# Longer GpSimd pieces in a fused recurrence and highway layer: up to 2,048 columns instead of 512, with a new list of operations

## The chip, the cores and the metric

The kernel runs on one core of a Trainium2 chip. The metric is the device time of one execution in microseconds. TensorE, VectorE, ScalarE, GpSimd and SyncE are the engines; the profile calls them PE (PEld for its weight loads), DVE, ACT, POOL and SP.

## What is computed

The input is 4 sequences of 6,336 tokens with 256 channels. A gated recurrence runs along each sequence, and a highway layer follows on all 25,344 tokens:

```python
sig = 1.0 / (1.0 + np.exp(-f_logit))
f = lower_bound + (1.0 - lower_bound) * sig
i = 1.0 - f
for t in range(S):
    h = f[:, t] * h + i[:, t] * x[:, t]
    y[:, t] = h
# on all tokens, with x = y
H = np.maximum(x @ w_h, 0.0)
T = 1.0 / (1.0 + np.exp(-(x @ w_t + b_t)))
out = T * H + (1.0 - T) * x
```

All inputs and the output are fp32 in DRAM.

## The kernel before

**Units.** The tokens are cut into 28 units in order (`units`, L42): two of 256 tokens, one of 512, twenty-three of 1,024, then 512 and 256. A unit has up to 8 blocks of 128 tokens. A tile first has tokens on the 128 partitions; for the recurrence it is turned, so that channels lie on the partitions (two halves of 128 channels, h = 0 and 1) and tokens along the columns.

**Operations.** Each has a letter, and a token of the list such as `b5.2:1` names the operation, the unit, a part of it and the buffer slot.

- `l`, `x` (L266, L269): loads of f_logit and x, issued by SyncE; six slots each.
- `u` (L272): ScalarE, sigmoid(-f_logit), fp16.
- `b` (L278, product at L283): u times x, into bv (bf16, two blocks interleaved). In pieces of 512 columns, four to a full unit; on GpSimd, or on VectorE where the token ends in v.
- `i` (L286): TensorE transposes u into PSUM (uT). `f` (L292): ScalarE makes f from it (L300), or VectorE with v (L298).
- `p` (L303, L309): TensorE transposes bv into PSUM (bT).
- `s` (L322, L326): VectorE's scan, y = f times the last y + bT, for 128 channels and a whole unit; it starts from the last column of the unit before. Where a sequence begins inside a unit there are two scans.
- `z`, `g` (L348, L351): TensorE's products of y with the two weight matrices (L343, L141). `t` (L354, L356): ScalarE, sigmoid of z. `d` (L358, L360): VectorE, one pass that reads y and g. In `y` the recurrence stands divided by a factor per channel, which diag and the scaled weights put back.
- `E`, `e` (L367, L370, product at L365): e = d times t over the 2 × tokens columns of the unit (both halves one behind the other). Columns below the last number of the unit's row in `units` are GpSimd's (`E`, pieces of 512), the rest VectorE's (`e`, one instruction).
- `o` (L376): TensorE turns four blocks back to tokens on partitions, summing y times diag (L384) and e times the identity (L385) in PSUM. `c` (L388): copy to SBUF, ScalarE (L394) or VectorE with v (L392). `w` (L398): store, issued by SyncE.

**Order.** The string `order` (L72 to L125) is the program: its tokens are emitted one after another, and each engine, SyncE's queue included, executes its own in that order. Semaphores make a token wait for its inputs and for its slot.

**GpSimd and VectorE.** `shared` (L204) adds one more wait. It is called with every VectorE product that has two SBUF inputs (`e`, `b` with v, the weight scaling at the start), and with every GpSimd product; the first GpSimd product listed behind such a VectorE instruction waits until that one is done.

```python
    def shared(ins, gpsimd):

        if not gpsimd:
            held[:] = [ins]
        elif held:
            tc.add_manual_dep(ins.ins, held.pop().ins.name, mybir.DependencyInfo(
                mybir.DependencyClass.Sync, mybir.DependencyReason.DATA), reason="shared port")
```

Of the kernel before, what the change touches and what calls it, by code (L numbers as in the profile page):

```python
# [19 lines left out]
def kernel(  # L20
# [70 lines left out]
g10.1:0 w7.1 i13.1:1 d10.1:2 b12.1 p11.1:0 s11.1 u15:2 g10.0:2 E9.2 o9.1:1 o9.0:0 f13.1:2 x15:2 E8.0 l14:3 b13.0:1
i12.0:1 b13.2 c9.1:1 w7.0 b13.3 i15.1:0 z11.0:1 b15.1:2 f12.0:0 p12.0:1 d10.0 z10.0:2 c9.0:2 x14:3 t11.0:0 o8.0:0
f15.1v:1 t10.0 w9.0 p12.1:0 b13.1 o8.1:2 s12.0:2 g11.1:1 c8.0:3 s12.1 i13.0:1 u14:0 E10.0:2 z12.1:0 b15.0 w9.1 d11.1:0
p13.1:0 z11.1:1 f13.0:0 i14.1:1 c8.1:0 e10 b14.1:0 w8.0 s13.1:0 g11.0:2 b14.2 t12.1:2 t11.1 l16:4 z12.0:0 b14.3
f14.1:3 w8.1 b14.0 x16:4 g12.0:1 t12.0 i14.0:0 p13.0:1 f14.0:2 d11.0 o10.0:2 d12.0:1 o10.1:1 c10.0:2 s13.0 l17:5
g12.1:0 E11.2:0 E11.0 E11.1 i15.0:1 p14.1:0 d12.1 c10.1:1 u16:1 z13.0:2 g13.0:0 e12:1 t13.0:1 f15.0:0 s14.1:1 o11.0:1
c11.0:3 E11.3 z13.1:2 p14.0:1 b16.3:1 b15.2 t13.1 b15.3 i16.0:0 f16.0:3 o11.1:1 d13.0:2 b16.0 g13.1:2 i16.1:0 w10.1
s14.0 c11.1:0 w10.0 p15.1:1 l20:0 d13.1 u17:0 w11.0 x17:5 b16.1 E12.0 s15.1:3 f16.1:2 z14.1:1 z14.0:0 b16.2 g14.1:2
d14.1:0 p15.0:1 l19:1 w11.1 i17.1:0 t14.1:0 E13.2:2 E13.3 s15.0 o12.1:2 E13.1 t14.0 g14.0:0 l18:2 x19:0 x18:1 u20:2
o12.0:1 c12.1:1 w12.1 d14.0 E13.0 p16.0:1 z15.0:2 b17.1:0 l21:3 f17.1:1 b17.0 b17.3 c12.0:2 E14.2:0 p16.1:0 t15.0:2  # L100
b17.2 s16.0:2 o13.1:1 g15.0:0 E14.1 i17.0:1 u19:1 o13.0:2 s16.1 f17.0:0 d15.0:1 p17.0:0 s17.0:0 g16.0:0 c13.0:3
c13.1:0 p17.1:1 u18:0 z15.1:1 E14.0 z16.1:2 E14.3 d16.0:2 i19.1:0 s17.1 g16.1:0 t15.1 w12.0 w13.0 x21:3 g15.1:1 d15.1
f19.1:3 w13.1 i18.0:0 i20.0:1 b19.1:2 b19.3 t16.1:1 g17.0:2 x20:2 b18.2:1 f18.0:2 i18.1:0 o14.0:1 b18.0 d16.1 d17.0:0
b18.3 b18.1 e15:1 E15.1 g17.1:0 o14.1:2 d17.1 b19.2 E15.0 f20.0:0 f18.1:1 c14.0:1 p18.1:1 u21:0 z16.0:1 z17.0:0
s18.1:1 t16.0 p18.0:0 o15.1:1 t17.0:0 b19.0 s18.0 b21.2:0 o15.0:0 c14.1:2 p19.1:1 z17.1:2 c15.1:3 e16:2 E17.1:0
b20.1:1 c15.0:0 i19.0:0 z18.1:1 b20.0 b20.3 l22:4 t17.1 b20.2 w14.0 g18.0:0 f19.0:1 z18.0:2 w14.1 p19.0:0 s19.1:3
E17.3 i20.1:1 d18.0:1 w15.1 t18.1:2 t18.0 o16.1:1 E17.0 g18.1:2 o16.0:0 b21.1 s19.0 d18.1 f20.1:2 w15.0 p20.0:1
i21.1:0 c16.1:1 z19.0:1 c16.0:2 E17.2 f21.1:3 x22:4 g19.1:0 b21.0 u22:1 b21.3 s20.0:2 z19.1:2 p20.1:0 i22.0:1 d19.1:2
s20.1 l23:5 t19.0:1 g19.0:0 o17.0:1 i21.0:0 f22.0:1 w16.1 t19.1 e18:1 g20.1:2 c17.0:3 f21.0:0 w16.0 d19.0 p21.0:1
o17.1:1 b22.1:2 b22.3 E19.1:2 d20.1:0 u23:2 p21.1:0 E19.2 z20.0:0 s21.0:0 o18.0:2 c17.1:0 t20.0:0 b22.0 z20.1:1  # L110
i23.1:1 x23:5 s21.1 b22.2 g20.0:0 c18.0:1 t20.1 o18.1:2 f23.1:2 d20.0 l24:0 p22.0:0 c18.1:2 w17.0 s22.0:1 i22.1:1
g21.0:1 z21.1:0 f22.1:0 i23.0:1 u24:0 b23.2:1 b23.1 p22.1:0 z21.0:2 d21.0:1 t21.1:2 E19.3 s22.1 g21.1:1 b23.0 E19.0
# [3 lines left out]
g23.1:1 c20.0:2 s24.1:2 i25.0:0 b25.3 z23.0:0 f25.0:3 z23.1:2 E21.1 i25.1:0 w20.1 b25.2 p24.0:1 t23.0:0 g23.0:0 t23.1
d23.1:0 o21.0:2 E22.0:2 w20.0 o21.1:1 E22.2 f25.1:2 c21.0:3 s24.0 E22.1 p25.0:0 x27:2 d23.0 c21.1:0 z24.0:2 x26:3
E22.3 z24.1:1 u26:2 s25.0:0 g24.1:0 p25.1:1 t24.0:2 d24.1:1 s25.1 t24.1 i26.0:0 f26.0:0 o22.0:2 o22.1:1 E23.0:0
g24.0:0 i26.1:0 b26.1:1 c22.0:1 b26.0 c22.1:2 d24.0 u27:0 z25.0:2 i27.0:1 e23 e24:1 g25.0:1 f26.1:1 z25.1:0 d25.0:2
w21.0 t25.0:1 E24.0 p26.1:0 o23.0:2 f27.0:3 E24.1 p26.0:1 o24.0:1 t25.1 w22.0 g25.1:0 c23.0:3 w21.1 b27.0:0 s26.1:1  # L120
# [71 lines left out]
    def tokens(n):  # L192
        return units[n][1] * units[n][2]

    def pieces(n):

        at, N = units[n][3], tokens(n)
        cuts = [0] + [c - at for c in firsts if at < c < at + N] + [N]
        return [(at + c in firsts, c, e) for c, e in zip(cuts, cuts[1:])]
# [240 lines left out]
```

## Time and profile before

The time before is 210.31 us (median of 3 runs, 210.30 to 210.35). The profile is of one execution whose span, from the first to the last instruction, is 208.8 us; 1.5 us lie around it.

| group | engine | count | mean ns of one |
|---|---|---|---|
| bv of 512 columns, L283 | GpSimd | 96 | 1,179 |
| e of 512 columns, L365 | GpSimd | 54 | 1,168 |
| scan of 1,024 tokens, L326 | VectorE | 40 | 2,336 |
| d of 1,024 tokens, L360 | VectorE | 46 | 1,263 |
| e of 2,048 / 1,536 / 1,024 / 512 columns, L365 | VectorE | 4 / 4 / 5 / 3 | 1,208 / 984 / 758 / 459 |
| bv of 512 columns, L283 | VectorE | 3 | 731 |
| copy o of 512 columns, L392 | VectorE | 1 | 665 |
| copy o of 1,024 columns, L394 | ScalarE | 48 | 1,057 |
| f of 1,024 tokens, L300 | ScalarE | 45 | 1,164 |
| u of 2,048 columns, L275 | ScalarE | 23 | 1,954 |

A mean is the length of one record. Records of one engine overlap a little, so the distance from one start to the next is shorter (a scan of 2,336 ns is followed 2.26 us after its start). The busy time counts overlapping time once. Lines of the profile's groups read: line, engine, operation, output <- inputs, shape, count | busy us, mean ns | idle time of the engine just before them, with what ended it. Lines of a timeline read: start, length, engine, line, operation, count, and in brackets the idle time before it. A digit in the slices is the busy share of a fortieth of the span, in tenths.

### The profile page before, as it was taken

The page shows a single profiled execution, that of the slowest core. Times are in us where ns is not written, and L with a number is a line of the kernel's source. Part 1 is how long each engine was busy: PE and PEld are TensorE (multiplying, and loading weights), DVE is VectorE, ACT ScalarE, POOL GpSimd, SP SyncE. Part 2 cuts the span into 40 slices and gives each one's busy share as a digit, 9 for nine tenths or more (in the row PEclk, how much of TensorE's full clock was granted, in tenths as well). Part 3 has the DMA queues.
Part 4 walks back from the last instruction along what each step waited for, and adds up shares of the span by engine and source line. Part 5 has one row for each costly group of instructions (what it writes and reads, how often), then busy time and mean ns, then how long its engine had stood idle before and what let it go on. Part 6 is the DMA issues. An engine that isn't in the chain of part 4 may idle for free.

```text
span 208.8 us, 4668 instructions
## 1 busy us (share of the span) xinstructions
PE 192.3 (92%) x1827; PEld 132.6 (64%) x1827; DVE 194.4 (93%) x154; ACT 195.0 (93%) x191; POOL 171.7 (82%) x162
## 2 busy tenths in 40 slices
PE   7888787989999999999999989999999999999991
PEld 2355455577675765776675766777677577776870
DVE  0799998999999999999999999999999999999970
ACT  4769979999999999999999999999999999999882
POOL 3076989789999399998799999879979988997920
PEclk9999999999999999999999999999999999999997
DMA  5999999999999999999999999999998999926676
GB/s 230 391 427 414 416 422 424 414 410 425 415 426 409 419 399 336 392 417 317 425 413 403 417 416 421 432 408 421 421 428 350 342 372 400 333 110 257 248 296 258
DMA packets 15982, 78.69 MB, mean 377 GB/s; under 512 B 1748, under 2 KB 2264, under 8 KB 10072
## 3 DMA queue, kind: packets, MB, share of 16 engines
q1 hardware_dynamic: 15952, 78.39, 93.6%
q8 instruction: 14, 0.23, 0.4%
q14 instruction: 8, 0.07, 0.1%
q10 hardware_dynamic: 8, 0.00, 0.0%
HBM read 52.43 MB, written 25.95 MB: 375 GB/s over the span
## 4 chain that ended last, share of the span: by engine, by line
PE 44%; DMA 17%; DVE 15%; ACT 12%; issue 5%; POOL 3%; SPq 2%; ACTq 0%; DVEq 0%; POOLq 0%
DMA l<-in_f_logit_dram 13%; DVE y L326 9%; PE op L385 6%; PE z L343 6%; PE op L384 6%; PE g L343 6%; PE z L141 5%; PE bT L309 5%; PE uT L289 5%; PE g L141 5%; DVE d L360 4%; ACT f L300 4%; DMA x<-in_x_dram 4%; ACT o L394 3%; ACT u L275 2%
## 5 line engine op out<-in xcount | busy, mean ns | idle before, releaser
L283 POOL TENSOR_TENSOR bv<-u,x 128x512 bf16<-128x512 f16 x96 | 110.3, 1179 | 21.7 <-DMA x<-in_x_dram 9.6
L326 DVE TENSOR_TENSOR_SCAN y<-f,y,bT 128x1024 bf16<-128x1024 f16 (+5 forms) x54 | 106.7, 1991 | 1.1 <-ACT f L300 0.5
L365 POOL TENSOR_TENSOR e<-d,t 128x512 bf16<-128x512 bf16 (+1 forms) x55 | 62.5, 1159 | 7.6 <-DVE e L365 4.5
L360 DVE SCALAR_TENSOR_TENSOR d<-y,ncc,g 128x1024 bf16<-128x1024 bf16 (+2 forms) x56 | 63.0, 1140 | 1.1 <-PE g L343 0.9
L300 ACT ACTIVATE f<-uT,ncc 128x1024 f16<-128x1024 f16 (+2 forms) x53 | 56.4, 1073 | 3.0 <-PE uT L289 2.9
L356 ACT ACTIVATE t<-z,bt 128x1024 bf16<-128x1024 f32 (+2 forms) x56 | 57.2, 1060 | 0.6 <-PE z L141 0.2
L394 ACT COPY o<-op 128x1024 f32<-128x1024 f32 (+1 forms) x50 | 50.7, 1038 | 2.2 <-PE op L385 1.4
L275 ACT ACTIVATE u<-l 128x2048 f16<-128x2048 f32 (+2 forms) x28 | 48.8, 1748 | 2.9 <-DMA l<-in_f_logit_dram 2.9
L384 PE MATMUL op<-diag,y 128*128 128x128 f16 x396 | 49.4, 219 | 1.9 <-ACT t L356 1.3
L385 PE MATMUL op<-ident_b,e 128*128 128x128 bf16 x396 | 49.3, 219 | 0.8 <-DVE e L365 0.6
L385 PEld LDWEIGHTS <-e 128*128 128x128 bf16 x396 | 44.0, 113 | 6.4 <-issue 2.9
L384 PEld LDWEIGHTS <-y 128*128 128x128 bf16 x396 | 44.2, 113 | 2.3
L343 PE MATMUL g<-y,w_sb 128*128 128x512 bf16 (+1 forms) x112 | 39.2, 367 | 0.8 <-DVE d L360 0.4
L343 PE MATMUL z<-y,w_sb 128*128 128x512 bf16 (+1 forms) x112 | 39.0, 367 | 0.4 <-DVE d L360 0.4
L309 PE MATMUL bT<-ident_f,bv 128*128 128x128 f32 x198 | 32.0, 279 | 4.2 <-ACT f L300 2.4
L141 PE MATMUL g<-y,w_sb 128*128 128x512 bf16 x92 | 34.9, 379 | 0.0
L141 PE MATMUL z<-y,w_sb 128*128 128x512 bf16 x92 | 34.9, 379 | 0.0
L289 PEld LDWEIGHTS <-u 128*128 128x128 f16 x396 | 26.1, 98 | 12.3 <-issue 3.7
L289 PE MATMUL uT<-ident_h,u 128*128 128x128 f16 x396 | 30.6, 219 | 2.7 <-DVE y L326 2.0
L343 PEld LDWEIGHTS <-w_sb 128*128 128x128 f16 x224 | 21.8, 98 | 15.8 <-issue 0.4
L309 PEld LDWEIGHTS bT<-ident_f,bv 128*128 128x128 f32 x198 | 22.2, 141 | 12.6 <-DVE y L326 3.1
L141 PEld LDWEIGHTS <-w_sb 128*128 128x128 f16 x184 | 18.0, 98 | 16.7 <-issue 2.1
(41 smaller groups left out, 52.4 us busy)
## 6 DMA issues: line engine op xcount, KB each, us to landing
out_dram<-o SPq DMA_DIRECT2D x48, 512.0 KB, 7.0
l<-in_f_logit_dram SPq DMA_DIRECT2D x23, 1024.0 KB, 11.3
x<-in_x_dram SPq DMA_DIRECT2D x23, 1024.0 KB, 10.1
l<-in_f_logit_dram SPq DMA_DIRECT2D x2, 512.0 KB, 7.1
x<-in_x_dram SPq DMA_DIRECT2D x2, 512.0 KB, 5.5
l<-in_f_logit_dram SPq DMA_DIRECT2D x3, 256.0 KB, 5.5
x<-in_x_dram SPq DMA_DIRECT2D x3, 256.0 KB, 4.9
out_dram<-o SPq DMA_DIRECT2D x3, 256.0 KB, 5.6
```

What stands on the lines that cost most here:

```text
L141: return pe.add_instruction(mybir.InstMatmult(name=nc.get_next_instruction_name(), start_tensor_calc=start, stop_tensor_calc=stop, tile_si ...
L283: shared(pin(e.tensor_mul(st[n]["bv"][:, k].rearrange("p d j -> p j d"), st[n]["u"][:, q:q + 2], st[n]["x"][:, q:q + 2])), not eng)
L289: pin(nc.tensor.transpose(uT[:, j * P:(j + 1) * P], st[n]["u"][:, j, h * P:(h + 1) * P], ident_h))
L300: pin(nc.scalar.activation(to, of, AF.Identity, scale=ncc[:, h:h + 1], bias=1.0))
L309: pin(nc.tensor.transpose(words[:, k:k + g * (P - 1) + 1:g], pair, ident_f))
L326: pin(nc.vector.tensor_tensor_scan(y[:, c:e], st[n]["f", h][:, c:e], st[n]["bT", h][:, c:e], 0.0 if fresh else carry[h], op0=ALU.mult, op1 ...
L343: pin(nc.tensor.matmul(p[:, a:e], w, half(n, "y", ki)[:, a:e], start=ki == 0, stop=ki == NH - 1))
L356: pin(nc.scalar.activation(half(n, "t", m), st[n]["z", m][:, :tokens(n)], AF.Sigmoid, bias=bt[:, m:m + 1]))
L360: pin(nc.vector.scalar_tensor_tensor(half(n, "d", m), half(n, "y", m), ncc[:, m:m + 1], st[n]["g", m][:, :tokens(n)], op0=ALU.mult, op1=AL ...
L365: shared(pin(eng.tensor_mul(st[n]["e"][:, a:e], st[n]["d"][:, a:e], st[n]["t"][:, a:e])), eng is nc.gpsimd)
L384: pin(nc.tensor.matmul(o, half(n, "y", h)[:, cols], diag[:, h], start=True, stop=False))
L385: pin(nc.tensor.matmul(o, half(n, "e", h)[:, cols], ident_b, start=False, stop=True))
```

## The change

A `b`, `E` or `e` token now names its first and its last piece of 512 columns (`b5.0-4`), and one instruction does them all:

```diff
-    def do_b(n, k, eng, slot):
+    def do_b(n, k, eng, slot, end):
         if "bv" not in st[n]:
             st[n]["bv"] = sb([P, NB // 2, D, 2], BF16, "bv", slot)
-        q = 2 * k
+        blk = slice(2 * k, 2 * end)
         e = nc.vector if eng else nc.gpsimd
-        shared(pin(e.tensor_mul(st[n]["bv"][:, k].rearrange("p d j -> p j d"), st[n]["u"][:, q:q + 2],
-                                st[n]["x"][:, q:q + 2])), not eng)
+        shared(pin(e.tensor_mul(st[n]["bv"][:, k:end].rearrange("p k d j -> p k j d"),
+                                st[n]["u"][:, blk].rearrange("p (k j) d -> p k j d", j=2),
+                                st[n]["x"][:, blk].rearrange("p (k j) d -> p k j d", j=2))), not eng)
...
-    def do_E(n, k, eng, slot):
-        times(n, nc.gpsimd, k * 512, min(units[n][6], k * 512 + 512), slot)
-
-    def do_e(n, k, eng, slot):
-        times(n, nc.vector, units[n][6], NH * tokens(n), slot)
+    def do_E(n, k, eng, slot, end):
+        times(n, nc.gpsimd, k * 512, end * 512, slot)
+
+    def do_e(n, k, eng, slot, end):
+        times(n, nc.vector, k * 512, end * 512, slot)
```

The rows of `units` keep only the first token and the number of blocks. The list is a new one throughout. What it holds differs in these counts:

| | before | after |
|---|---|---|
| `b` on GpSimd | 96 of 512 columns | 4 of 512, 4 of 1,024, 2 of 1,536, 20 of 2,048 |
| `b` on VectorE | 3 of 512 (b0.0, b3.3, b3.0) | 1 of 512 (b0.0) |
| `E` on GpSimd | 54 of 512, 1 of 256; 27,904 columns | 16 of 512, 4 of 1,024, 2 of 1,536, 10 of 2,048; 35,840 columns |
| `e` on VectorE | 17 instructions, 22,784 columns | 12 instructions, 14,848 columns: 2 of 512, 5 of 1,024, 3 of 1,536, 2 of 2,048 |
| `c` on VectorE | 1 (c1.0) | 5 (c1.0, c2.0, c9.1, c23.1, c27.0) |
| `f` on VectorE | 3 (f0.1, f2.1, f15.1) | 2 (f0.1, f2.0) |

The first lines and the last of the new list, for its form and for its two ends:

```diff
+l0:0 l3:1 pc:0 wh u0:0 i0.0:0 i0.1:1 k*10 l1:2 x0:0 wt cc dg f0.1v:0 f0.0:1 x1:1 u3:1 u1:2 i1.0*5:0 WH b0.0-1v:0 l2:3
+x2:2 f1.0:2 p0.1*2:1 b1.0-1:1 i1.1:0 x3:3 l4:4 s0.1:0 p0.0:1 s0.0 f1.1:3 p1.1*2:0 p1.0:1 g0.0:1 s1.1:1 u2:0 i2.1:0
+b2.0-2:2 WTa s1.0 i2.0:1 d0.0:0 f2.1:0 f2.0v:1 g0.1:0 x4:4 i3.1:0 d0.1 l5:5 f3.1:3 g1.1:2 z0.0:1 p2.1:1 t0.0:0 s2.1:2
+z0.1:0 t0.1 i3.0:0 l7:0 p2.0*1:1 g1.0:1 f3.0:2 z1.0:0 d1.1:1 b3.0-4:0 u4:2 s2.0 g2.1:2 d1.0 z1.1:1 x5:5 E0.0-1:0
...
+E25.3-4 E25.2-3 c24.1:3 p27.1:1 p27.0:0 w24.1 z26.1:0 d26.0:2 t26.1:2 o23.1:2 z26.0:1 s27.1:1 o25.1:0 t26.0 s27.0
+z27.0:1 c23.1v:2 g26.1:1 z27.1:1 o25.0:2 E26.0-1:0 c25.1:0 t27.0:0 g27.1:0 c25.0:1 w23.1 d26.1 w25.1 g27.0:0 e26.1-2
+o26.0:0 w25.0 d27.0:0 d27.1 t27.1 e27.0-1:1 o27.0:1 c27.0v:3 c26.0:2 w26.0 w27.0
```

More of the change, by code (lines that the diff above doesn't have):

```diff
@@ L91 @@
[L91 to L100, printed above, removed]
@@ L116 @@
[L116 to L120, printed above, removed]
@@ L121 @@
-w22.1 i27.1:0 c24.0:1 o24.1:2 s26.0 p27.0:1 f27.1:2 d25.1 w23.0 p27.1:0 E23.1 z26.1:1 s27.0:2 w24.0 E25.0:2 c24.1:0
-o23.1:0 z26.0:2 s27.1 t26.1:2 c23.1:2 z27.1:1 z27.0 e25 g26.0:1 w24.1 d26.0:1 t26.0 o25.1:0 w23.1 E26.0:1 t27.1:0
-g26.1:2 d26.1 c25.1:3 o25.0:1 w25.1 c25.0:1 g27.0:0 g27.1 e26 w25.0 d27.1:0 t27.0 o26.0:0 d27.0 c26.0:0 e27:0 o27.0:1
-w26.0 c27.0:2 w27.0
+l0:0 l3:1 pc:0 wh u0:0 i0.0:0 i0.1:1 k*10 l1:2 x0:0 wt cc dg f0.1v:0 f0.0:1 x1:1 u3:1 u1:2 i1.0*5:0 WH b0.0-1v:0 l2:3
+x2:2 f1.0:2 p0.1*2:1 b1.0-1:1 i1.1:0 x3:3 l4:4 s0.1:0 p0.0:1 s0.0 f1.1:3 p1.1*2:0 p1.0:1 g0.0:1 s1.1:1 u2:0 i2.1:0
@@ new lines @@
+x7:1 c2.0v:2 p5.0:1 s5.1:1 u8:0 z4.0:1 g4.0:0 i6.1:0 t4.1:1 b6.0-4:0 w1.0 s5.0 t4.0 l10:3 o3.0:2 g4.1:1 x8:2 f6.1:0
+l9:4 c3.0:3 i7.1:1 i8.1:0 z5.1:2 d4.0:1 d4.1 e4.0-2:1 f7.1:1 p6.1:1 f8.1:3 o3.1:0 i6.0:0 t5.1:2 w3.0 e4.2-4 g5.0:1
+c3.1:0 f6.0:2 s6.1:2 z5.0:2 p6.0:1 o4.0:0 u10:2 c4.0:1 d5.0:2 s6.0 i7.0:0 f7.0:0 x9:3 b7.0-4:1 t5.0 g5.1:1 p7.1:1
+g6.1:0 l12:5 d5.1 i8.0:0 s7.1:3 u9:1 f8.0:2 g6.0:1 b8.0-4:2 o4.1:2 p7.0:1 E5.0-4:2 i9.0:0 c4.1:3 d6.1:0 z6.1:0 f9.0:1
+z6.0:2 p8.0:0 t6.1:0 s7.0 w2.0 i9.1:1 z7.0:0 t6.0 f9.1:0 w4.1 l11:0 b9.0-4:0 o5.0:2 t7.0:1 d6.0 E6.0-4:0 p8.1:1 x10:4
@@ new lines @@
+s8.0:0 s8.1 z7.1:1 g7.1:0 i10.1:0 c5.0:2 g7.0:2 d7.1:1 t7.1 u12:0 f10.1:2 o5.1:1 p9.1:1 d7.0 z8.1:0 b10.0-4:1 i12.1:0
+w5.0 c5.1:3 g8.1:2 t8.1:2 s9.1:1 z8.0:1 p9.0:1 w4.0 g8.0:0 d8.1:2 f12.1:3 t8.0 l15:1 x11:5 o6.0:2 E7.0-4:1 u11:1
+o6.1:1 p10.1:0 w3.1 c6.0:2 s9.0 d8.0 s10.1:2 i11.1:1 z9.1:2 c6.1:1 f11.1:0 g9.1:0 d9.1:0 t9.1:0 l13:2 i10.0:1 f10.0:1
+z9.0:1 t9.0 b11.0-4:2 p10.0:0 E8.0-2:2 s10.0 i11.0:1 g9.0:2 o7.1:0 o7.0:1 d9.0 e8.2-4 f11.0:2 e9.0-3:0 w6.1 p11.1:1
+u13:2 E9.3-4 z10.1:2 c7.1:0 w6.0 s11.1:3 x12:0 i13.1:0 o9.0:0 x13:1 b12.0-4:0 c7.0:1 w7.0 w5.1 g10.1:1 p11.0:1 f13.1:1
@@ new lines @@
+c9.0:2 t10.1:1 i12.0:0 d10.1:1 z10.0:0 o9.1:1 g10.0:2 s11.0 b13.0-3:1 c9.1v:1 u15:1 d10.0 f12.0:0 w7.1 p12.1:1 i15.1:0
+s12.1:1 z11.1:1 t10.0 z11.0:0 l14:3 f15.1:2 b13.3-4 p12.0:0 t11.1:2 o8.1:2 s12.0 g11.1:1 t11.0 d11.1:2 i13.0:1
+E10.0-4:1 o8.0:0 x14:2 p13.1:0 u14:0 f13.0:3 l16:4 c8.1:3 i14.1:1 c8.0:0 s13.1:0 g12.1:1 g11.0:2 d11.0 w9.0 b14.0-4:2
+z12.1:0 f14.1:0 u16:2 x15:3 t12.1:0 E11.0-4:0 d12.1:0 i14.0:0 p13.0:1 g12.0:2 w9.1 s13.0 f14.0:1 d12.0 w8.1 o10.0:1
+c10.0:2 o10.1:0 c10.1:1 i15.0:0 l17:5 f15.0:3 p14.1:1 w10.0 z12.0:1 x16:4 o11.1:0 s14.1:2 b15.0-4:0 t12.0 g13.1:2
@@ new lines @@
+d13.1:1 c11.1:3 i16.0:0 p14.0:1 f16.0:0 s14.0 w10.1 o11.0:1 u17:0 E12.0-2:2 g13.0:0 c11.0:2 z13.0:2 i16.1:0 p15.1:1
+e12.2-4 w8.0 o12.0:1 d13.0 t13.0:1 f16.1:1 c12.0:1 z13.1:2 z14.1:0 b16.0-2:1 p15.0:0 o12.1:1 t13.1 t14.1:2 g14.1:2
+c12.1:0 l20:0 u20:1 g14.0:0 s15.1:3 s15.0 d14.1:2 b16.2-4 i17.1:1 z15.0:1 E13.0-4:1 d14.0 x17:5 p16.1:0 s16.1:1 w11.1
+z15.1:2 f17.1:2 l18:2 z14.0:0 t15.0:0 p16.0:1 s16.0 b17.0-3:2 t15.1 b17.3-4 g15.0:1 t14.0 i17.0:0 E14.0-3:0 o13.1:2
+d15.0:0 l19:1 w11.0 E14.3-4 f17.0:3 o13.0:0 p17.0:0 c13.1:3 x18:0 u18:2 p17.1:1 s17.0:0 g16.0:2 z16.1:1 u19:0 d16.0:1
@@ new lines @@
+l21:3 c13.0:2 i19.1:0 w13.0 g15.1:2 f19.1:1 g16.1:0 x19:1 s17.1 i18.0:0 w13.1 i18.1:1 t16.1:1 d15.1 g17.0:1 d16.1
+d17.0:2 b18.0-4:0 f18.0:0 f18.1:3 i20.0:0 w12.0 e15.1-4:2 f20.0:2 o14.1:2 g17.1:0 p18.0:1 c14.1:2 x20:2 w12.1 o14.0:1
+u21:2 d17.1 z16.0:2 z17.1:0 p18.1:0 E15.0-1 t16.0 c14.0:3 z17.0:2 t17.1:2 s18.0:2 i19.0:1 b19.0-4:1 t17.0 o15.1:1
+s18.1 w14.0 c15.1:1 e16.0-3:1 E16.3-4 o15.0:0 b20.0-4:2 p19.1:0 s19.1:3 l22:4 E17.0-4:0 f19.0:0 c15.0:0 z18.0:2
+z18.1:1 p19.0:1 o16.1:0 t18.1:0 s19.0 i20.1:0 g18.0:1 t18.0 d18.0:0 w15.1 x21:3 c16.1:3 g18.1:2 p20.0:1 u22:0 l23:5
@@ new lines @@
+f20.1:3 o16.0:0 g19.1:1 d18.1 z19.0:2 c16.0:1 i21.1:0 s20.0:1 z19.1:0 t19.0:1 f21.1:1 d19.1:1 p20.1:1 o17.0:2 i22.0:0
+w16.0 x22:4 t19.1 f22.0:0 s20.1 g19.0:1 w15.0 o17.1:0 c17.0:1 b21.0-4:0 i21.0:0 E19.3-4:2 f21.0:2 u23:1 d19.0
+e18.0-4:1 b22.0-4:1 c17.1:0 g20.1:2 z20.0:1 p21.1:1 t20.0:2 d20.1:2 o18.0:2 w17.0 x23:5 s21.1:0 p21.0:0 z20.1:0 s21.0
+i23.1:1 w17.1 c18.0:1 l24:0 g20.0:1 o18.1:2 f23.1:3 E19.0-3 d20.0 p22.0:1 w14.1 b23.0-4:2 w18.0 t20.1 i22.1:0 x24:0
+s22.0:2 c18.1:0 z21.1:0 f22.1:1 g21.0:1 E20.0-4:0 z21.0:2 t21.1:0 t21.0 d21.0:0 l25:2 p22.1:0 i23.0:1 g21.1:0 w16.1
@@ new lines @@
+i26.1:0 b26.0-2:2 t24.1 s25.1 E24.3-4:0 o22.0:0 E24.2-3 w21.0 c22.1:2 u27:2 d24.0 e23.0-4:1 z25.0:2 p26.1:1 f26.1:0
+i27.0:0 g25.0:1 c22.0:3 f27.0:2 d25.0:1 x27:3 w21.1 w22.0 w22.1 t25.0:1 E24.0-1 z25.1:0 p26.0:0 o23.0:2 t25.1 o24.0:1
+g25.1:0 c23.0:0 w23.0 c24.0:1 s26.0:2 s26.1 E24.1-2 b27.0-1:0 w24.0 i27.1:0 E25.0-2:2 f27.1:3 d25.1 g26.0:2 o24.1:1
+E25.3-4 E25.2-3 c24.1:3 p27.1:1 p27.0:0 w24.1 z26.1:0 d26.0:2 t26.1:2 o23.1:2 z26.0:1 s27.1:1 o25.1:0 t26.0 s27.0
+z27.0:1 c23.1v:2 g26.1:1 z27.1:1 o25.0:2 E26.0-1:0 c25.1:0 t27.0:0 g27.1:0 c25.0:1 w23.1 d26.1 w25.1 g27.0:0 e26.1-2
@@ L192, in tokens @@
     def tokens(n):
-        return units[n][1] * units[n][2]
+        return units[n][1] * P
     def pieces(n):
-        at, N = units[n][3], tokens(n)
+        at, N = units[n][0], tokens(n)
         cuts = [0] + [c - at for c in firsts if at < c < at + N] + [N]
@@ L276, in do_u @@
         st[n]["u"] = u
-    def do_b(n, k, eng, slot):
+    def do_b(n, k, eng, slot, end):
         if "bv" not in st[n]:
             st[n]["bv"] = sb([P, NB // 2, D, 2], BF16, "bv", slot)
-        q = 2 * k
+        blk = slice(2 * k, 2 * end)
         e = nc.vector if eng else nc.gpsimd
-        shared(pin(e.tensor_mul(st[n]["bv"][:, k].rearrange("p d j -> p j d"), st[n]["u"][:, q:q + 2],
-                                st[n]["x"][:, q:q + 2])), not eng)
+        shared(pin(e.tensor_mul(st[n]["bv"][:, k:end].rearrange("p k d j -> p k j d"),
+                                st[n]["u"][:, blk].rearrange("p (k j) d -> p k j d", j=2),
+                                st[n]["x"][:, blk].rearrange("p (k j) d -> p k j d", j=2))), not eng)
     def do_i(n, h, eng, slot):
         uT = one_bank(slot, FP16, "uT")
-        for j in range(units[n][2]):
+        for j in range(units[n][1]):
             pin(nc.tensor.transpose(uT[:, j * P:(j + 1) * P], st[n]["u"][:, j, h * P:(h + 1) * P], ident_h))
@@ L410 @@
         n, _, k = name[1:].partition(".")
-        here["do_" + name[0]](int(n), int(k or 0), token.endswith("v"), slot)
+        k, _, end = k.partition("-")
+        span = (int(end),) if end else ()
+        here["do_" + name[0]](int(n), int(k or 0), token.endswith("v"), slot, *span)
 _INS = ['x', 'f_logit', 'lower_bound', 'moe_w_h', 'moe_w_t', 'moe_b_t']
```

81 lines of the change are left out of this document (14 added, 67 removed), and 4 rows, old and new, of the table units.

## The prediction

> **What bounds the kernel now.** I read the busy table first, then the slices, then the list of groups by shape, then the timelines of VectorE and GpSimd beside each other.
>
> ```profile
> span 208.8 us, 4668 instructions
> PE 192.3 (92%) x1827; PEld 132.6 (64%) x1827; DVE 194.4 (93%) x154; ACT 195.0 (93%) x191; POOL 171.7 (82%) x162
> DVE  0799998999999999999999999999999999999970
> ACT  4769979999999999999999999999999999999882
> POOL 3076989789999399998799999879979988997920
> DMA  5999999999999999999999999999998999926676
> ```
>
> Three engines are busy for 92% or 93% of the span and the DMA engines for most of it. The slices tell them apart: VectorE loses its time at the two ends. Its timeline has a first part to 25 us with waits (0.45 and 0.49 us for TensorE's bT, and shorter ones), then one gap of 0.53 us at 34.6, and after that it runs back to back until 199.2 us. So the recurrence, the d pass, the products e and the copies that VectorE executes, one after another, set the time; ScalarE is almost as full, with more small gaps. GpSimd is free for 37 us, but much of that is forced, as the timeline of both engines at one place shows.
>
> ```profile
> 128.55 4.56 POOL L283 TENSOR_TENSOR bv<-u,x 128x512 bf16<-128x512 f16 x4 [0.21 <-ACT f L300]
> 133.73 1.16 POOL L365 TENSOR_TENSOR e<-d,t 128x512 bf16<-128x512 bf16 x1 [0.62 <-DVE e L365]
> ...
> 132.68 0.97 DVE L365 TENSOR_TENSOR e<-d,t 128x1024 bf16<-128x1024 bf16 x1
> 133.58 1.27 DVE L360 SCALAR_TENSOR_TENSOR d<-y,ncc,g 128x1024 bf16<-128x1024 bf16 x1
> 169.07 0.69 DVE L365 TENSOR_TENSOR e<-d,t 128x1024 bf16<-128x1024 bf16 x1
> ```
>
> GpSimd's four pieces ended at 133.11. VectorE's e was started at 132.68 and took 0.97 us, against 0.69 us for the same shape at 169.07: it lost 0.28 us to GpSimd's running piece. Then GpSimd stood until e was done, because `shared` (L204) makes the first GpSimd instruction behind a VectorE product wait for it. So the two engines meet at every VectorE product, and between two meetings each does its own list. Only pieces listed ahead of e can stand in its way: e waits out GpSimd's lateness, not a random rest of a piece, however long the pieces are.
>
> The Trainium skill has this as a rule (SBUF — State Buffer, Who interferes with whom): a VectorE instruction with two SBUF inputs and a GpSimd instruction that reads SBUF exclude each other for the whole of whichever came first. The 0.28 us above agrees. Without `shared` this rule would speak against the change: an estimate for ten products that each meet a long piece at its middle is 10 × 2.0 = 20 us, where the sum below has 0.7.
>
> **GpSimd's price.** Here is the price of a longer piece, which before never executes.
>
> ```profile
> L365 POOL TENSOR_TENSOR e<-d,t 128x512 bf16<-128x512 bf16 x54 | 61.8, 1168 | 7.6 <-DVE e L365 4.5 <-DVE d L360 2.4 <-DVE bv L283 0.7
> L365 POOL TENSOR_TENSOR e<-d,t 128x256 bf16<-128x256 bf16 x1 | 0.7, 677 | 0.0
> ...
> 108.47 2.29 POOL L283 TENSOR_TENSOR bv<-u,x 128x512 bf16<-128x512 f16 x2
> 110.72 0.68 POOL L365 TENSOR_TENSOR e<-d,t 128x256 bf16<-128x256 bf16 x1
> 111.35 1.17 POOL L283 TENSOR_TENSOR bv<-u,x 128x512 bf16<-128x512 f16 x1
> 112.47 1.16 POOL L365 TENSOR_TENSOR e<-d,t 128x512 bf16<-128x512 bf16 x1
> ```
>
> From start to start, 512 columns take 1.12 us (111.35 to 112.47) and 256 columns 0.63 us (110.72 to 111.35). The difference, 0.49 us for 256 columns, is 1.9 ns a column, which leaves 0.145 us that each piece pays once. An estimate for 2,048 columns is 0.145 + 2,048 × 1.9 ns = 4.04 us, for 1,024 2.09, for 1,536 3.06. There is a single 256-column row, so the bounds are wide. Upper: nothing saved, four times 1.12 = 4.47 us. Lower: 512-column records lie between 1.15 and 1.22 us; if the 256-column one is off by as much (0.03 us) the slope is 1.78 ns and the long piece 3.85 us. I take 4.04, the only value that two neighbouring rows give.
>
> The Trainium skill (GPSIMD Engine Reference, 3.1) gives 4,497 ns for a two-input add of 2,048 fp32 columns, and 2.6 cycles a column as the floor for two inputs. By it the sum would come to about the 219.7 us of the first rival below instead of 208.4. The row of 256 columns speaks against it, at 1.9 ns (2.3 cycles at the page's 1.2 GHz) a column.
>
> Counts from the two lists: GpSimd's b goes from 96 pieces to 30 (4, 4, 2 and 20 of 512, 1,024, 1,536 and 2,048 columns), E from 55 to 32 (16, 4, 2, 10), and E's columns from 27,904 to 35,840. By the prices above GpSimd's work was 150 × 1.12 + 0.63 = 168.6 us and becomes 20 × 1.12 + 8 × 2.09 + 4 × 3.06 + 30 × 4.04 = 172.6 us. The columns cost more than the merging saves, but 17 VectorE products, at each of which GpSimd stood, become 12. Does the longer list still fit between the meetings? I add both engines' work between one VectorE product and the next, in us, with scan 2.26 and d 1.18 start to start. Before, the large stretches are 20.2 (VectorE) and 20.1 (GpSimd), 26.6 and 25.7, 28.9 and 28.6, 15.0 and 14.5, 13.8 and 13.4: GpSimd is done just ahead each time. After, by the same prices: 28.5 and 27.7, 34.7 and 34.4, 27.7 and 27.6, 23.0 and 20.6, 5.7 and 5.2, 14.0 and 14.3, 20.7 and 20.3, 13.8 and 13.5, 8.4 and 8.8. Only two stretches have GpSimd late, by 0.3 and 0.4 us. **+0.7 us.**
>
> **VectorE's work.** Records overlap the next by 0.09 us, so each instruction counts its mean less 0.09.
> - Products e: before 4 × 1.208 + 4 × 0.984 + 1.092 + 5 × 0.758 + 3 × 0.459 = 15.0 us; after two of 2,048, three of 1,536, five of 1,024 and two of 512 columns, 10.1 us; with five fewer overlaps, **-4.5 us**.
> - f15.1 moves to ScalarE (one record of 1.273): **-1.2 us**.
> - Copies o: one of 512 columns stays (0.665). c2.0, c9.1 and c23.1 of 1,024 columns and c27.0 of 512 come. No row shows 1,024 columns on VectorE. Below, nothing would bound it but ScalarE's 1.057; above, twice 0.665 = 1.33. The d group, which also reads PSUM, grows by 527 ns from 512 to 1,024 columns, so I take 1.19, net 1.10: 3 × 1.10 + 0.58 = **+3.9 us**. c27.0 only takes the place of ScalarE's last copy (0.59 us at 204.39) on the last chain: **-0.6 us** back.
> - Two bv pieces of unit 3 (2 × 0.64 us) go to GpSimd, at the start. There VectorE waits anyway. GpSimd was ready for unit 3 at 14.9, needs 4.04 us for all of it, and ends at 18.96; before, VectorE's own last piece ended at 18.22 + 0.74 = 18.96. The scan behind it (19.83) starts no earlier. Only the d of unit 2 is done in the hole, and GpSimd's next bv ends at about 24.1 instead of 24.76, so the scan of unit 4, 25.25 now, comes 0.25 us sooner: **-0.25 us**, not 1.28.
>
> **Other engines.** ScalarE loses three copies of 1.057 and one of 0.582 and gains one f of 1.164: -2.6 us of 195.0. It has to keep step with VectorE, and can. TensorE's list has the same instructions in another order; in a full stretch it shows 0.22 us a 512-column product and gaps. The DMAs are the same 78.69 MB; at the 420 GB/s of the full slices that is 187 us, and the last loads are issued at 178.6, before the end by 30 us, so there is cover. SyncE's writes w9.1 and w23.1 now wait for a VectorE copy. Behind w9.1 stand other writes and loads, but it is listed some 10 us behind its copy. Behind w23.1 stand the last four writes, which wait for later copies themselves.
>
> **Sum.** -4.5 - 1.2 + 3.9 - 0.6 - 0.25 + 0.7 = -1.95 us. The profiled span of 208.8 becomes 206.85; the median of the runs, 210.31, lies 1.5 us above the span, so **208.4 us**.
>
> **Rivals.**
> - *Long pieces save nothing, and GpSimd becomes the bound* (slower). At 4.19 us a piece the stretch sums, with max of the two engines in each, come 2.9 us above those at 4.04, which is more than the gain; at 4.47 us GpSimd's list is 187 us and the sums come 11.3 us higher. The gain is lost from about 4.16 us on. It gives 211 to 219.7 us; halfway between the bounds, 213. For it: one row alone carries the slope, and back-to-back pieces show no gap that merging could remove. Against it: that row says the same twice (677 ns, and 0.63 us to the next start). Chance 0.27. The skill's figure for 2,048 columns stands on this rival's side.
> - *Lateness eats the gain.* A long e piece needs both halves of d and t, where a 512-column one needed one half; a wait inside a stretch has 0.1 to 0.8 us of room in most. If each of the ten meetings before the tail costs 0.2 us more (one above cost 0.28), that is 2 us: 210.3, no change. Chance 0.13.
> - *More comes back.* VectorE's gap at 34.6 and its lost time at meetings (about 0.8 us over the 17) go, and c23.1 fits into the 0.9 us that VectorE waits behind the last scan: 1.5 to 2 us more, 206.6. Chance 0.08.
> - *The change does less than it says*: the built lists show 62 GpSimd products instead of 151 and five VectorE copies, so I give this nothing.
>
> The forecast itself, 207.2 to 209.8, has 0.52. What a measurement of this kernel can tell from no change is about 0.2%, 0.4 us. Faster 0.60, within 0.10, slower 0.30. The range runs from the third rival to halfway in the first, 206.6 to 213.
>
> **What would show it.** The mean of the 2,048-column GpSimd rows: 4.1 us confirms, 4.4 refutes. VectorE's busy time should fall by about 3 us to 191, without new gaps; a product e that is longer than 0.69 (1,024 columns) or 1.21 us (2,048) would show lateness. GpSimd's busy time should come to 175 or so. Copies on VectorE of 1.2 us. I am wrong if TensorE or a load shows up in front of VectorE's scans.

## The result and the profile after

The changed kernel takes 217.93 us (median of 4 runs, 214.79 to 219.12) against 210.31. A ratio here leaves out runs that lie more than 1.5% above the kernel's fastest: it rests on the runs of 214.79 and 217.35 us (mean 216.07), not on the profiled one of 218.5, though the clock is 0.996 to 0.998 in all four. So the ratio is 1.028, with an interval of 1.022 to 1.034: **slower by 2.8%** (by 3.6% with the median of all runs). 208.4 was forecast, and the range ended at 213.

The page of the changed kernel, busy table, slices and queue first:

```profile
span 216.7 us, 4545 instructions
PE 191.7 (88%) x1799; PEld 133.2 (61%) x1827; DVE 194.9 (90%) x150; ACT 193.1 (89%) x188; POOL 175.8 (81%) x73
DVE  1688999999999999999998999998899889979971
ACT  4689999999999999989979999787987999889871
DMA  6999999998999999999999979999799999993776
```

GpSimd's busy time is what was forecast (175 or so). VectorE's is not: 191 was forecast. Its row of slices, solid nines before, has 7s and 8s in six slices from the 22nd on, before its end, and ScalarE's has still more of them in the same half. So something stops both. The DMA row, which had one 8 before it came to the last loads, now has a 7 in the 24th and in the 29th slice. The list of waits tells what is late; first before, then after (total us, times, longest):

```profile
POOL bv L283 <- DMA x<-in_x_dram: 9.6, 3, 7.7
ACT u L275 <- DMA l<-in_f_logit_dram: 2.9, 4, 1.0
```
```profile
POOL bv L254 <- DMA x<-in_x_dram: 15.9, 8, 7.7
ACT o L366 <- DMA out_dram<-o: 5.3, 5, 1.4
DVE y L298 <- PE bT L281: 5.1, 8, 1.0
ACT u L246 <- DMA l<-in_f_logit_dram: 4.5, 8, 1.1
```

The longest wait for x (7.7) is the start in both. The rest is new. Loads of x are late at five more places and loads of f_logit at four. The second line did not exist: the copy `c` finds its o buffer still being read by the store that left it. The third is what follows at VectorE, whose scan waits for TensorE's bT (0.9 us at two places before). Of its five stops behind the start, bT is late behind ScalarE's copies or f at 154.89, 170.78 and 182.84, behind GpSimd's late bv at 190.78, and behind other work of TensorE at 194.75. The chain that ended last, followed back from the last instruction, goes through seven stores out of o, for 32% of the span; before, it goes through none.

Where is the time lost? Three scans that both kernels have, before first, give the progress (start, length). The single scans of 640 and 448 columns stand where a sequence begins, the last line is the last pair:

```profile
104.73 1.46 DVE L326 TENSOR_TENSOR_SCAN y<-f,bT 128x640 bf16<-128x640 f16 x1
148.59 1.06 DVE L326 TENSOR_TENSOR_SCAN y<-f,bT 128x448 bf16<-128x448 f16 x1
197.00 1.38 DVE L326 TENSOR_TENSOR_SCAN y<-f,y,bT 128x256 bf16<-128x256 f16 x2
```
```profile
102.52 1.46 DVE L298 TENSOR_TENSOR_SCAN y<-f,bT 128x640 bf16<-128x640 f16 x1
151.68 1.06 DVE L298 TENSOR_TENSOR_SCAN y<-f,bT 128x448 bf16<-128x448 f16 x1
205.20 1.38 DVE L298 TENSOR_TENSOR_SCAN y<-f,y,bT 128x256 bf16<-128x256 f16 x2
```

At half way the changed kernel leads by 2.2 us, the size of the gain that was forecast. Then it falls behind by 3.1 and at the end by 8.2 us: it loses 10.4 us in its second half.

One place of that loss in the changed kernel's timeline:

```profile
132.07 8.06 SPq L371 DMA_DIRECT2D out_dram<-o  x2
140.18 0.95 SPq L234 DMA_DIRECT2D l<-in_f_logit_dram  x1
...
137.30 4.12 POOL L254 TENSOR_TENSOR bv<-u,x 128x2048 bf16<-128x2048 f16 x1 [1.56 <-PE z L112]
138.76 1.01 ACT L366 COPY o<-op 128x1024 f32<-128x1024 f32 x1 [1.29 <-DMA out_dram<-o]
140.02 2.22 DVE L337 TENSOR_TENSOR e<-d,t 128x1536 bf16<-128x1536 bf16 x1
```

The copy stands 1.29 us for a store out of its buffer, which was issued at 129.51 and landed at 138.74. SyncE issues a store at 132.07 and then stands for the store of that very copy, whose end is at 139.77. So the next load, l, is issued only at 140.18; it lands at 149.37, and ScalarE's u stands 1.09 us for it. And a VectorE product e takes 2.22 us, against 0.95 for this shape in experiment 10 below: a GpSimd piece that began late runs to 141.42 beside it. The x of that piece was issued at 129.07 and landed at 137.14, 0.06 us before the z that the line names.

What in the list makes this? I laid the stores and copies of both lists on VectorE's work (each of its instructions counted from its start to the next). From a copy to its store there are 4.6 us in the old list (mean; 12.8 at most) and 8.4 in the new one (28.6 at most). From a store to the next copy into the same one of four o buffers there are **9.1 us in the old list and 5.1 in the new**. In 13 of 47 such pairs the old list has less than 7 us, and the new one in 33. A store lands 7.0 us (before) or 6.7 us (after) after its issue by the median, and 14 to 15 at most. So on average the old list leaves room for a store and the new one doesn't. The real times in the traces show the order behind it: before, a store is issued 0.2 us after the end of its copy on average, and 2 of 51 wait longer than 2 us; in the changed kernel it is 3.8 us, and 18 of 51 wait longer than 2 us, because the stores no longer stand in the order in which their copies end (17 stand behind a store whose copy ended over 1 us later; 3 before). It is 3.7 us in experiment 10 too, where more buffers bear it.

### The profile page after: what moved, and what is told of

Same layout as the page of the kernel before. It is cut to its first block, busy times and chain, and to the rows that moved or that the text cites. A ratio compares the mean times of both kernels' runs of the same rounds, so it can differ in the third digit from the quotient of the medians.

```text
span 216.7 us, 4545 instructions
## 1 busy us (share of the span) xinstructions
PE 191.7 (88%) x1799; PEld 133.2 (61%) x1827; DVE 194.9 (90%) x150; ACT 193.1 (89%) x188; POOL 175.8 (81%) x73
## 3 DMA queue, kind: packets, MB, share of 16 engines
q1 hardware_dynamic: 15952, 78.39, 93.5%
## 4 chain that ended last, share of the span: by engine, by line
DMA 44%; PE 22%; ACT 10%; DVE 8%; issue 8%; SPq 3%; POOL 2%; ACTq 0%; DVEq 0%; POOLq 0%
DMA out_dram<-o 32%; DMA x<-in_x_dram 11%; ACT o L366 6%; DVE y L298 5%; PE z L315 4%; PE g L315 3%; PE bT L281 3%; PE op L356 3%; PE op L357 3%; PE z L112 3%; PE uT L261 2%; POOL bv L254 2%; SPq L234 2%; PE g L112 2%; DVE d L332 2%
## 5 line engine op out<-in xcount | busy, mean ns | idle before, releaser
L254 POOL TENSOR_TENSOR bv<-u,x 128x2048 bf16<-128x2048 f16 (+3 forms) x30 | 101.8, 3402 | 25.7 <-DMA x<-in_x_dram 15.9
L337 POOL TENSOR_TENSOR e<-d,t 128x512 bf16<-128x512 bf16 (+3 forms) x32 | 73.9, 2315 | 6.7 <-DVE e L337 5.3
L272 ACT ACTIVATE f<-uT,ncc 128x1024 f16<-128x1024 f16 (+2 forms) x54 | 57.3, 1067 | 3.6 <-PE uT L261 2.9
L366 ACT COPY o<-op 128x1024 f32<-128x1024 f32 (+1 forms) x46 | 46.5, 1031 | 9.1 <-DMA out_dram<-o 5.3
L315 PE MATMUL z<-y,w_sb 128*128 128x512 bf16 (+1 forms) x112 | 39.5, 367 | 2.3 <-ACT o L366 1.5
L281 PE MATMUL bT<-ident_f,bv 128*128 128x128 f32 x198 | 31.4, 277 | 4.4 <-DVE y L298 2.2
L261 PEld LDWEIGHTS <-u 128*128 128x128 f16 x396 | 26.0, 98 | 12.3 <-issue 3.7
L112 PE MATMUL z<-y,w_sb 128*128 128x512 bf16 x80 | 30.3, 379 | 0.0
L112 PE MATMUL g<-y,w_sb 128*128 128x512 bf16 x78 | 29.5, 379 | 0.0
```

Source lines behind the costliest of these rows:

```text
L112: return pe.add_instruction(mybir.InstMatmult(name=nc.get_next_instruction_name(), start_tensor_calc=start, stop_tensor_calc=stop, tile_si ...
L254: shared(pin(e.tensor_mul(st[n]["bv"][:, k:end].rearrange("p k d j -> p k j d"), st[n]["u"][:, blk].rearrange("p (k j) d -> p k j d", j=2) ...
L261: pin(nc.tensor.transpose(uT[:, j * P:(j + 1) * P], st[n]["u"][:, j, h * P:(h + 1) * P], ident_h))
L272: pin(nc.scalar.activation(to, of, AF.Identity, scale=ncc[:, h:h + 1], bias=1.0))
L281: pin(nc.tensor.transpose(words[:, k:k + g * (P - 1) + 1:g], pair, ident_f))
L315: pin(nc.tensor.matmul(p[:, a:e], w, half(n, "y", ki)[:, a:e], start=ki == 0, stop=ki == NH - 1))
```

## The experiments

The theories at the start were S, the places of the stores in the list; P, the long pieces; and D, the DMA engines being full. Q, B and C came later. Q: the loads stand behind stores that wait for copies. B: the transfers as a whole take too long, in whatever order. C: a copy waits for the last store out of its buffer, and its own store then holds the loads behind it, so that more output buffers help. Ratios are to the kernel before on the same chip, whose median was 210.20 to 210.37.

**1. The long pieces alone.** The old list, in which neighbouring GpSimd pieces are put together, with nothing else moved (16 b and 7 E of 2,048 columns; 67 GpSimd products instead of 151):

```diff
-b4.2:1 b4.1 t1.0:1 b4.0 p3.1:0 t1.1 i4.1:1 b4.3 f4.1:1
+t1.0:1 p3.1:0 t1.1 i4.1:1 b4.0-4:1 f4.1:1
```

> The list of before, with GpSimd's pieces of one unit joined where no VectorE product and no reader stands between (16 of the b and 7 of the E become 2,048 columns long; 67 GpSimd products instead of 151); VectorE's work, the loads and the stores stay where they were. Theory S (the new list puts its stores off, so that copies wait for buffers): 209 to 211 us, as before. Theory P (long pieces make GpSimd's readers late): 213 us or more, with waits of TensorE's bT for GpSimd. Theory D (the DMA engines are full, and a kernel that is faster on its engines cannot be fed): 210 to 211 us.

Measured: 211.21 us, ratio 1.0046 (1.0031 to 1.0061). GpSimd's busy time falls from 171.7 to 159.8 us. The long pieces by themselves cost 1 us, not 8: P is not the cause. GpSimd waits for x for 14.3 us at nine places here, nearly as long as in the changed kernel, since one long piece needs the whole x; so a longer wait for x does not by itself tell a loss.

**2. The stores earlier.** The new list with 27 stores moved forward towards their copies, by 9 us of VectorE's work on average. Of SyncE's tokens:

```diff
-l11:0 x10:4 w5.0 w4.0 l15:1 x11:5 w3.1 l13:2 w6.1 w6.0 x12:0 x13:1 w7.0 w5.1
+l11:0 x10:4 w5.0 l15:1 x11:5 w5.1 w6.0 l13:2 w6.1 x12:0 x13:1 w7.0
```

> The new list, with each store moved forward to about 3.5 us of VectorE work behind its copy; nothing else moves, on no other queue. Theory S: 207 to 212 us, and ScalarE's copies no longer wait for stores (5.3 us now). Theory P: no change, 214 to 219. Theory D: no change or slower, 214 to 221, since the loads then stand behind more stores.

Measured: 227.82 us (223.69 to 228.38, without a ratio), slower than the changed kernel: the two ranges lie 4.6 us apart. Its waits:

```profile
POOL bv L254 <- DMA x<-in_x_dram: 20.2, 9, 7.8
ACT u L246 <- DMA l<-in_f_logit_dram: 11.5, 10, 3.1
```

A store that is nearer to its copy stands longer at the head of the one queue (SyncE waits 141 us for ScalarE's copies, at 39 stops, where the changed kernel has 121 us at 27), and the loads behind it come later: l costs 11.5 us instead of 4.5, x 20.2 instead of 15.9. The copies' wait for stores is 4.6 us. In the form "the stores are too late, so move them forward" (S, 207 to 212 us) the theory fell; D's 214 to 221 was too low as well.

**3 and 4. Lighter stores.** In the changed kernel and in the kernel before, each store writes only half of its blocks of tokens, so half of the output stays unwritten and 65.70 MB move instead of 78.69:

```diff
-        pin(nc.sync.dma_start(rows(out, n, j0, j1), st[n]["o", q][:, :j1 - j0]))
+        pin(nc.sync.dma_start(rows(out, n, j0, j1)[:, :(j1 - j0) // 2], st[n]["o", q][:, :(j1 - j0) // 2]))
```

> The changed kernel, in which each store writes half of its blocks (the other half of the output is left unwritten; 65.7 MB move instead of 78.7). The engines' work and all waits stay. Theories S and D: 207 to 210 us, what the prediction's sum gave, since copies and loads wait for transfers no longer. Theory P: 213 us or more, since the pieces stay long.

> The kernel before with the same cut (each store writes half of its blocks, the rest of the output is left unwritten). All theories: 209 to 210.3 us, since its engines set the time; a fall below 208 would say that transfers held it too.

Measured: 207.39 us (ratio 0.987, 0.984 to 0.990) for the changed kernel and 209.00 (0.994, 0.992 to 0.995) for the old one. No copy waits for a store any more, and VectorE's busy time is 191.4 us, as forecast. So the loss comes from transfers, and all of it: relieved of them, the changed kernel is 1.6 us faster than the old one under the same relief. A half store moves fewer bytes and also lands sooner (4.0 us instead of 6.5), so this alone does not tell the amount of the transfers from their order; 10 does.

**5, 6 and 7. The loads earlier.** Loads are issued 23 to 29 us on average after their buffer is free, in both kernels, so there is room. In the new list 30 loads are moved forward by up to 12 us of VectorE's work, or 34 by up to 22; in the old one 36 by up to 22. The stores keep their places.

```diff
-l11:0 x10:4 w5.0 w4.0 l15:1 x11:5 w3.1 l13:2 w6.1 w6.0 x12:0 x13:1
+x10:4 l11:0 w2.0 w4.1 x11:5 w5.0 w4.0 l13:2 l15:1 w3.1 x12:0 x13:1 w6.1 w6.0
```

> The new list with the loads of units 10 to 27 moved forward in SyncE's queue, to 12 us of VectorE work ahead of their first reader where their buffer is free by then (3 us forward on average). Nothing else moves. Theory Q (the loads stand behind stores that wait for copies, so that the transfer queue runs dry and loads land late): 209 to 214 us, with fewer waits of GpSimd for x (15.9 us now, 8 of them in the start). Theory B (the transfers as a whole take too long in whatever order): 215 to 219, as the changed kernel.

> The same with 22 us ahead of the first reader (9 us forward on average). Theory Q: 207 to 210 us, what the prediction's sum gave. Theory B: 215 us or more, since now stores are late, and copies wait for their buffers.

> The list of before with the same move of its loads (22 us ahead, 9 us forward on average). Both theories: 209 to 210.5 us if its loads land in time already; under B perhaps slower, where stores are held back and copies wait for buffers.

Measured: 227.21 us (1.080, 1.075 to 1.085) and 231.08 (1.096, 1.090 to 1.101) on the new list, 213.71 (1.017, 1.015 to 1.018) on the old one, where the copies now wait 3.2 us for stores. The further the loads move, the worse: Q's forecasts (209 to 214, then 207 to 210) fell. The first of the waits of the kernel with 22 us:

```profile
ACT o L366 <- DMA out_dram<-o: 20.1, 11, 4.4
```

The loads of x are in time again (9.8 us at three places, 8.1 of it the start). Instead the copies wait for the stores, 20.1 us in place of 5.3. Over all stores the time from issue to landing has not grown by the median (6.6 us), but the eleven stores that were waited for took 11.0 us on average and were issued 6.7 us after their copy's end; for the five of the changed kernel it is 10.1 and 7.9. The two longest took some 17 us, with five and eight loads issued in the 13 us ahead of them, where the five had one to four. Part of the slowness of 2, 5 and 6 comes over the clock: behind stands of TensorE of 2.3 to 5.3 us the clock that it is granted is 0.5 for 3.4 or 6.8 us, two to four times in each profile, while the changed kernel shows this at its end alone. Experiments 2, 5 and 6 are two sides of one thing: with four o buffers, what helps the loads in the new list hurts the stores, and the other way round.

**8 and 9. More output buffers.** Seven o buffers instead of four, in both lists; the copies take the one that is free longest. The space comes from the sixth l buffer and from w_raw, which is used only at the start. Nothing else moves.

```diff
-w_raw = sb([P, 2, NH, D], FP32, "w_raw")
+w_raw = sb([P, 2, NH, D], FP32, "w_raw", "o6")
...
-c3.0:3 c3.1:0 c4.0:1 c4.1:3
+c3.0:3 c3.1:4 c4.0:5 c4.1:6
```

> The new list, operation by operation, with seven buffers for the copies o instead of four (f_logit's buffers go from six to five, and the weights' first tile shares one of the seven). Theory C (each copy waits for its buffer's last store, which stands some 7 us in the transfer queue; the store behind the copy then holds the loads behind it): 207 to 212 us, and ScalarE's copies wait for no store. Theory B (the transfers as a whole take too long): 215 to 219 us.

> The list of before with the same seven buffers. Theories B and C: 209.5 to 210.5 us, since its copies wait for no store with four.

Measured: 215.68 us (1.018, 1.012 to 1.024) for the new list, 210.07 (0.9987, 0.9978 to 0.9997) for the old one. No copy waits for a store in either. But in the new list the loads are later than ever:

```profile
POOL bv L254 <- DMA x<-in_x_dram: 21.4, 9, 7.7
ACT u L246 <- DMA l<-in_f_logit_dram: 7.3, 9, 1.7
```

Buffers alone give back some 2 us, less than the runs of either kernel spread (212.98 to 216.43 here, 214.79 to 219.12 without them). This is slower than C said (207 to 212) and where B put it (215 to 219). With the copies free to run, the late loads are what is left.

**10 and 11. Both.** The seven o buffers of 8 with the earlier loads of 5 and of 6.

```diff
-l11:2 x10:4 w5.0 w4.0 l15:3 x11:5 w3.1 l13:4 w6.1 w6.0 x12:0 x13:1
+x10:4 l11:2 w2.0 w4.1 x11:5 w5.0 w4.0 l13:3 l15:4 w3.1 x12:0 x13:1 w6.1 w6.0
```

> The new list with seven buffers and with the loads moved forward to 12 us ahead of their first reader (227.2 us with four buffers, copies waiting 13.0 us for stores). Theory C: 206.5 to 210 us, the prediction's sum, with neither copies nor GpSimd waiting for transfers behind the start. Theory B: 215 us or more.

> The same with the loads 22 us ahead (231.1 us with four buffers). Theory C: 206.5 to 212 us; seven buffers may be too few again where stores are held back furthest. Theory B: 215 us or more.

Measured: **207.94 us (0.9888, 0.9873 to 0.9903) and 207.90 (0.9887, 0.9873 to 0.9902)**. Either change alone leaves the new list at 215.7 or at 227 to 231 us, and together they beat the kernel before by 2.4 us, with the same bytes moved. These are C's forecasts (206.5 to 210, and to 212), and B's 215 or more is out. The page of the first:

```profile
span 206.0 us, 4538 instructions
...
PE 189.4 (92%) x1799; PEld 132.7 (64%) x1827; DVE 191.6 (93%) x150; ACT 192.0 (93%) x188; POOL 175.6 (85%) x73
...
DVE  0678999999999999999999999999999999999972
...
DMA  6999999999999999999999999999999999962776
```

VectorE's row is solid again and its busy time is what the forecast said, 191.6 us; DMA has no hole ahead of its last loads. The copies' wait for stores is gone from the list, and of the waits for x, l and bT these are left (GpSimd's 7.7 us at the start are put down to ScalarE's f here):

```profile
POOL bv L254 <- DMA x<-in_x_dram: 2.9, 3, 1.3
...
ACT u L246 <- DMA l<-in_f_logit_dram: 2.0, 5, 0.6
...
DVE y L298 <- PE bT L281: 1.7, 4, 0.6
```

**12 and 13. The cross-checks on the old list.** First, 31 stores of the old list put off by 2 to 14 us of VectorE's work (5.5 on average), so that 5.5 us are left from a store to the next copy into its buffer, as in the new list; loads, pieces and engines stay. Second, the whole remedy (seven buffers, loads up to 22 us earlier) on the old list. The edit of the first, of SyncE's tokens:

```diff
-w5.1 x11:5 x12:0 w5.0 l13:1 l15:2 w6.1 w6.0 x13:1
+x11:5 w5.1 x12:0 l13:1 l15:2 w5.0 w6.1 w6.0 x13:1
```

> The list of before with its stores of units 5 on put off, so far that by VectorE's work 5.5 us on average lie between a store and the next copy into its buffer (9.1 us before, 5.1 us in the new list); nothing else moves. Theory C, if the stores' place is enough by itself: 213 to 220 us, with copies that wait for stores. If the new list's loads or its faster engines are needed too: 210 to 212 us.

> The list of before with seven buffers for o and its loads moved forward by 9 us on average: what made the new list 10 us faster than the changed kernel. If the engines set the time of before, 209.5 to 210.3 us; if before is held by transfers too, 208 us, and then the remedy and not the change is worth the time.

Measured: 216.18 us (1.030, 1.025 to 1.035) for the first, 210.39 (1.0001, 0.9992 to 1.0011) for the second. The places of the stores alone make the old kernel as slow as the changed one. Its waits show how one late store spreads:

```profile
ACT o L394 <- DMA out_dram<-o: 4.6, 3, 4.1
PE z L343 <- ACT o L394: 4.3, 1, 4.3
...
DVE d L360 <- PE g L141: 5.9, 1, 5.9
```

ScalarE's copy stands 4.1 us for a store, TensorE's next z 4.3 us for that copy, and VectorE's d 5.9 us for TensorE. The waits for x stay as they were (9.7 us). So the form is not quite that of the changed kernel, where many short waits do the same; and behind TensorE's stand the granted clock is 0.5 for 3.4 us, which can add 1.7 us at most. The second run says that the gain of 10 and 11 is the change's and not the remedy's: on the old list the remedy is worth nothing.

## Why the prediction was wrong

**The step that failed** is the one on the DMAs and SyncE in "Other engines", which costed the transfers at nothing. It argued from the amount (78.69 MB, the same), from the issue of the last load (30 us of cover), and from two stores that now wait for a VectorE copy. In the changed kernel the amount is the same, the last load has 25 us of cover, and SyncE waits 10.7 us for VectorE's copies, as in the fast kernel of experiment 10 (10.6). So none of the three tells the slow kernel from the fast one. What it left out is that the new list re-sorts all 107 transfers of SyncE's one queue. Two counts from the list would have shown it: the room from a store to the next copy into its buffer, 5.1 us where 9.1 were, against a landing time of 7 us that the trace of before holds; and the loads that stand behind a store whose copy is late. The sentence "listed some 10 us behind its copy" was even taken as a good sign, while a store that is put off keeps its buffer for that long. (The store named there went out 0.03 us behind its copy, at 86.76: only its place among SyncE's own tokens counts, and others stand behind copies that end later.) No rival named it. Against the forecast's -1.95 us, the gain with the transfers in order is -2.4 us (experiment 10), and their disorder, which the sum had at nothing, costs +8.1 us by the ratio's runs (216.07 less 207.94) and +10.0 by the medians.

**How the loss comes about**, as far as the runs show it. The room is too small, so copies wait for stores (5.3 us). SyncE executes in order, so a store that waits for its copy holds the loads behind it, and x and l come late (some 8 us more than before, though experiment 1 shows that some 5 us of that for x cost little by themselves). From there two ways lead to VectorE. One goes over ScalarE, whose late u, f and copies make TensorE late: of the 10.7 us between the profiled spans of the changed kernel and experiment 10, 7.4 are idle time of VectorE, with 5.1 us against 1.7 in the wait for bT. Its waits for g were 2.7 us against 0.2, but their stops were not followed one by one. The other goes over GpSimd, which gets x late and ends its pieces late, so that VectorE's e stands behind them. VectorE's products show this second way; here are the same five instructions in the changed kernel and in experiment 10:

```profile
L337 DVE TENSOR_TENSOR e<-d,t 128x1024 bf16<-128x1024 bf16 x5 | 5.0, 1012 | 0.0
```
```profile
L337 DVE TENSOR_TENSOR e<-d,t 128x1024 bf16<-128x1024 bf16 x5 | 3.8, 769 | 0.0
```

One of the five took 2.20 us, beside GpSimd's pieces, which had stood 1.59 us for two late x; the others took 0.67 to 0.86. All its e together are 12.3 us in the one and 10.4 in the other (10.1 forecast). That is 1.9 of the 3.3 us by which VectorE's busy time exceeds that of experiment 10; the list of waits doesn't name this loss, since the engine counts as busy. That the places of the transfers are the cause is shown, by 2, 5 to 8 and 10 to 12 together. How much of the loss goes through late copies and how much through late loads stays open: each of them turned into the other when it alone was relieved.

**The steps that held.**

- *GpSimd's price.* 4.04 us was taken for 2,048 columns, from one 256-column row; b takes 4.12 and E 4.08 by the rows below. GpSimd's list is 175.8 us busy where 175 were forecast. The first rival, which rested on 4.19 to 4.47, is out: the slower time that it gave was of the right sign for a wrong reason.

```profile
L254 POOL TENSOR_TENSOR bv<-u,x 128x2048 bf16<-128x2048 f16 x20 | 82.4, 4123 | 13.2 <-DMA x<-in_x_dram 6.9 <-ACT f L272 2.0 <-PE z L112 1.6
L337 POOL TENSOR_TENSOR e<-d,t 128x2048 bf16<-128x2048 bf16 x10 | 40.8, 4084 | 0.0
L364 DVE COPY o<-op 128x1024 f32<-128x1024 f32 x3 | 3.6, 1203 | 0.0
```

The 256-column row was within 2%. The Trainium skill (GPSIMD Engine Reference, 3.1) gives 4,497 ns for fp32 at 2,048 columns; these bf16 and f16 products take 4,084 to 4,123, so the figure is 9 to 10% too long for them.

- *Copies on VectorE.* 1.19 us was an estimate from the d rows; three copies took 1.20.
- *Meetings.* The forecast said that e waits out GpSimd's lateness and not a random rest of a piece. In experiment 10 the five e of 1,024 columns average 0.77 us, 0.08 over the clean 0.69, and one of 2,048 took 1.67 where the other took 1.22: lateness there is small, as the stretch sums had it. In the changed kernel the five average 1.01.
- *The sum.* -1.95 us from 210.3, so 208.4; 207.9 with the transfers in order, and a difference of -1.6 us where both kernels move less. Right as a statement on the engines, which is not what was asked.
- *What was to refute it.* "I am wrong if TensorE or a load shows up in front of VectorE's scans" is what the third line of the waits shows.

## What to carry to other kernels

When a hand-written order is replaced, read the transfers like an engine: for each store, how much work lies from it to the next writer of its buffer, against the landing time in the trace; for each load, which stores stand ahead of it in the queue and what they wait for. The amount of bytes and the last load say nothing about this. When a loss moves from stores to loads as one of them is helped, look for the resource they share, here the four buffers and one queue in order, and relieve both at once. A second queue for the stores, which would part them from the loads, was not tried here.

## What the runs showed of the hardware

- A GpSimd product of two inputs costs nearly by the column over the whole range here: 1.15, 2.14, 3.11 and 4.08 us for E of 512, 1,024, 1,536 and 2,048 columns. Merging four pieces saves some 0.4 us (four starts of 1.12 us against 4.08).
- The DMA share hardly shows a queue that runs dry. q1's packets take 93.5% in the changed kernel and 93.6% before, in a span that is 8 us longer. Single packets got longer. An 8 KB packet takes mostly 0.309 us, and the time above that (0.159 us for 4 KB ones), summed and spread over the 16 engines, is some 7 us before, 14 after and 7 in experiment 10. It is 14 in experiment 3 too, which is fast, so it does not measure the loss either. Some of the long ones stand right behind stretches in which the DMA engines were busy for 25% to 59% only (128 to 130 and 152 to 154 us in the changed kernel). Whether that is their cause was not tried, and five or six o buffers were not tried either.
- TensorE's granted clock fell to 0.5 for 3.4 or 6.8 us behind each stand of its matmuls of 2.3 to 5.3 us after the first 20 us (experiments 2, 5, 6 and 12). Stands of 1.8 us or less show no such stretch.
